# One read-back a tile instead of four, and five weights' low parts made by an adding transfer, in a fused S4 and SwiGLU kernel

## The chip, the cores and the metric

The kernel runs on one core of a Trainium2 chip. The metric is the device time of one execution in microseconds. The core has five engines with queues of their own: PE multiplies matrices, DVE and ACT work elementwise (both read PE's accumulator banks), POOL works elementwise on SBUF, and SP issues most of the transfers (DMA). 16 DMA engines move what SP, ACT and POOL issue. Instructions on one engine run in the order in which they were written; across engines they wait on semaphores.

## The reference

The input is 2048 tokens of width 448. A layer norm with modulation, a long convolution in the form of an S4 state space, and a residual come first; a second layer norm with modulation, a SwiGLU of hidden width 1792, and a second residual follow.

```python
mod = (_silu(c) @ w_mod).reshape(c.shape[0], 6, 1, -1)
sa, ca, ga, sb, cb, gb = (mod[:, 0], mod[:, 1], mod[:, 2], mod[:, 3], mod[:, 4], mod[:, 5])
h = _layernorm(x, axis=-1) * (1 + ca) + sa
x = x + ga * _A_ref(h, ...)          # y[l] = sum over m <= l of K[l - m] h[m], plus h * Dskip
h = _layernorm(x, axis=-1) * (1 + cb) + sb
x = x + gb * ((_silu(h @ w_gate) * (h @ w_up)) @ w_down)
```

## The kernel before

**Tiles and blocks.** The tokens make 16 tiles of 128; two tiles are a block, and there are 8 blocks. The input data let the convolution be done by running sums (the branch taken here; the other branch, for general data, is in the program but does not run). A prologue of about 34 us makes the modulation rows and the first block's input.

**A block** (ffn) runs 14 units f = 0 to 13, each of 128 hidden columns. A unit is gate_up (42 pairs of matmuls into two banks), point (the down products of the unit before, written between gate_up's matmuls at the position POINT), and gating (SiLU on ACT at L774, the product on DVE at L786, its high part on ACT at L791, its low part on DVE at L792). To keep accuracy, each operand is split into a high part, rounded for PE, and a low part, the rest; a product is high x high, high x low and low x high. hhi and hlo are the two parts of the block's turned tokens, phi and plo those of the gated product, wdh and wdl those of w_down, and gu holds both parts of a unit's gate and up weights. gate_up reads hhi with the weights' high part, hlo with the high part, and hhi with the low part; in block 0 the low part comes last.

**Weights.** All weights stay in SBUF. They are loaded and split in block 0 alone: load_w brings the weights of one unit into one of three buffers called raw (L104), split_w makes the high part on ACT (part 0, L121, a unit before its use and in gating) and the low part on DVE (part 1, L123, at the end of unit f for unit f + 2). split_d does the same for w_down.

**The next block's input.** While a block runs, the plan PLANS lists under each unit which steps of the next block's two tiles come there: for each tile X and Y (the second norm's two halves, make_xn at L207 and L209), T (turn) and U (turned_back). Steps marked + come ahead of the cast to phi in gating, the others behind it. turn transposes 32 x 32 pieces on DVE (L239) and SP copies the result to xd in DRAM (L240); turned_back reads it back with the pieces in their places, doubled for PE's two halves, into the buffer place[q] (a raw buffer that is free then), by four transfers of 32 partitions each (L245). In the last unit split_turned makes hhi (ACT, L252) and hlo (DVE, L253) from it, in two steps, LOW and HIGH. The next block's first matmuls need hhi of both tiles. In blocks 1 to 6 tile 0 has T and U under unit 8, tile 1 has X, Y, T and U under unit 10.

**Queues.** SP's order is that of the program: a transfer that waits holds back those written behind it. In block 0 the weight loads stand between the turned tokens' transfers; in later blocks the stores of the block before and the loads of x (L818, L87) stand behind them.

**The end.** In the last block the last two units' down products go to other banks (finish), the sums of the units before are scaled and added to x by last_sums (L832, L833), and three additions (L852) and the stores end the program.

Of the kernel before, what the change touches and what calls it, by code (L numbers as in the profile page):

```python
# [18 lines left out]
L, D, N, F = 2048, 448, 256, 1792  # L19
# [4 lines left out]
NF = F // 128  # L24
# [6 lines left out]

PLANS = (
    """pre: s0 t0 R0 ; mid: f ; g a0 s1 t1 R1 ; b0 G ; r0 h0 ; +v0 a1 c0 ; A0 p0 b1 ; B0 e0 E0 ; r1 h1 u0 w0 M0 ; +v1 X0 Y0 c1 p1 ; A1 T0 ;
    B1 E1 m1 M1 ; U0 X1 Y1 T1 ; U1 e1 ; L0 ; L1""",
    """n0 n1 N ; +l0 a0 b0 k0 ; +l1 k1 r0 h0 ; +v0 a1 b1 c0 ; A0 p0 ; B0 e0 E0 c1 ; r1 h1 m0 M0 p1 ; +v1 X0 Y0 L0 L1 ; A1 T0 U0 ; B1 E1 m1 M1 ; X1 Y1 T1 U1 ; e1 ; ;""",
    "; l0 k0 ; l1 k1",
)
POINT = ([12] + [20] * 12 + [12], [12] + [18] * 12 + [12])  # L40
ORDER = """sf x0 x1 sc m10 se sd m11 m20 m21 m00 m01 sb sa m40 m41 m30 m31 w0 m50 m51 w1 d0 d1 x2 w2 x3 d2"""

PLAN = """t4 pa0 t1 S1 t2 pa1 t3 wi ca gp S20 wr h00 gpc gt h01 mp S21 gac m0 dg gdm mpc k0 a2 t5 sq1 mk gdr h10 cp S3 v00 dga a3 o00
# [8 lines left out]
def f32(ap):  # L52
    return ap.bitcast(F32)
# [3 lines left out]
def tile_kernel(ctx, tc, x, a_re, a_im, b_re, b_im, c_re, c_im, log_dt,  # L57
                wd, wgate_up, states, groups, vecs, dft, idft, out):
    nc = tc.nc
    sy, ve, sc, po, pe = nc.sync, nc.vector, nc.scalar, nc.gpsimd, nc.tensor  # L60
# [5 lines left out]
    dram = ctx.enter_context(tc.tile_pool(name="dram", bufs=1, space=bass.MemoryType.DRAM))  # L66
# [24 lines left out]
    wgu, raw, wdn, wp = {}, {}, {}, {}  # L91
# [5 lines left out]
    place = [stages_[:, q].rearrange("p k c -> p (k c)") for q in (2, 0)]  # L97
# [20 lines left out]
    def split_w(j, part):  # L118
        w = raw[j]
        if part == 0:  # L120
            sc.copy(wgu[j][:, 0], w)  # L121
        else:
            ve.tensor_tensor(wgu[j][:, 1], w, f32(wgu[j][:, 0]), op=OP.subtract)  # L123

    tri = const.tile([128, 128], F32R)
    tok = const.tile([128, 1], F32)
# [66 lines left out]
    n1, n2 = Norm("a"), Norm("b")  # L193
# [37 lines left out]
        ve.tensor_scalar(i, j, 0.0, None, op0=OP.is_equal)  # L231
        return i

    xd = [dram.tile([128, D], F32, name=f"xd{q}") for q in range(2)]

    def turn(i, q):

        src, dst = h_of(i), v0_of(i)
        ve.transpose(dst.rearrange("p (b k r) -> p k b r", b=2, k=7), src.rearrange("p (k b c) -> p k b c", b=2, k=7))  # L239
        sy.dma_start(xd[q], dst)  # L240

    def turned_back(q):
        for z in range(4):
            b = z % 2
            sy.dma_start(place[q][z * 32:(z + 1) * 32].rearrange("c (a n) -> c a n", a=4),  # L245
                         xd[q][:, b * 224:(b + 1) * 224].rearrange("(a c) n -> c a n", a=4))

    def split_turned(ks):
        for q in range(2):
            src = turned[q].rearrange("p a k r -> p k a r")[:, ks]  # L250
            hi, lo = (h[:, ks, cols(q)].rearrange("p k (a r) -> p k a r", a=4) for h in (hhi, hlo))
            sc.copy(hi, src)  # L252
            ve.tensor_tensor(lo, src, f32(hi), op=OP.subtract)  # L253
# [40 lines left out]
    with tc.tile_pool(name="pre", bufs=1) as pre:  # L294
# [4 lines left out]
        for kind, q in ((n[0], n[1:]) for n in ORDER.split()):  # L299
# [3 lines left out]
            elif kind == "m":  # L303
                g, b = int(q[0]), (slice(0, 2 * D), slice(2 * D, NM))[int(q[1])]
# [36 lines left out]
        for z in range(2):  # L341
# [16 lines left out]
        m0, m0_, a1, a2, m1 = (pre.tile([128, 4], F32, name=q) for q in ("m0", "m0_", "a1", "a2", "m1"))  # L358
# [3 lines left out]
        h01, v0, v1, hd = ([pre.tile([128, w], t, name=f"{n}_{q}") for q in range(2)] for n, t, w in  # L362
                               (("h", F32, D), ("v0", F32, D), ("v1", F32R, D), ("hd", F32, D)))
# [116 lines left out]
        k0, k1 = CV[:, 0:D], DN[2][:, 0:D]  # L480
# [259 lines left out]
    def run_blocks(pools, stages, first=None):  # L740
# [13 lines left out]
        def ffn(b, ts, fresh, last, todo):  # L754
            n, sums = 256, SUMS[b % 2]
# [12 lines left out]
            def gating(f, ps, nw):  # L768
                p = hid.tile([128, 256], F32, name="p") if fresh else p_of[f % 2]
                hi = hid.tile([128, 256], F32R, name="phi")  # L770
                lo = hid.tile([128, 256], F32R, name="plo")
                for g, a in todo.get(-2, []) if f == 0 else []:
                    g(*a)
                gate_ready[:] = [sc.activation(p, ps[0][:, 0:n], AF.Silu).ins.name]  # L774
                pp[f] = hi, lo
                if f == NF - 1:
                    if fresh:
                        split_d(f, 1)
                    for q in range(3):
                        for o in [cols(q)] * (q < 2):  # L780
                            ve.tensor_tensor(p[:, o], p[:, o], ps[1][:, o], op=OP.mult)
# [10 lines left out]
                ve.tensor_tensor(lo, ps[1][:, 0:n], f32(hi), op=OP.subtract)  # L792
# [33 lines left out]
                po.tensor_tensor(raw, raw, gb, op=OP.mult)  # L826
                wdn[f] = raw

            def last_sums():

                for q, i in enumerate(ts):
                    ve.tensor_tensor(sums[q][:, 0:D], sums[q][:, 0:D], gb, op=OP.mult)  # L832
                    ve.tensor_tensor(xs[i], sums[q][:, 0:D], xs[i], op=OP.add)  # L833

            def finish():
                o = [*SUMS[1 - b % 2], bank()]
# [36 lines left out]
            for f in range(NF):  # L873
                ps, ops = gate_up(f)
                ops = list(zip(*ops))
                at = POINT[b > 0][f]
                both(ops[0][:at], ops[1][:at])
                point(f)
                both(ops[0][at:], ops[1][at:])
                if f == NF - 1 and not last:  # L880
                    split_turned(LOW)
                gating(f, ps, f + 2 if fresh and f + 2 < NF else None)
                if f == NF - 1 and not last:
                    split_turned(HIGH)
                if last and f in (2, 5):
                    gated(NF - 2 + (f == 5))
                if last and f in (4, 7):
                    split_d(NF - 2 + (f == 7))
                if last and f == NF - 1:
                    last_sums()  # L890
                    return finish()
                if fresh and f == 0 and first is None:
                    sy.dma_start(run[0:1], run[127:128])
                for g, a in todo.get(f, []):
                    g(*a)
                if fresh:
                    if f + 2 < NF:
                        split_w(f + 2, 1)
                    pools.load(f + 2 + NS, f + NS)
            ahead[:] = [begin]  # L900

# [229 lines left out]
```

## Time and profile before

| | |
|---|---|
| time, median of 3 runs | 471.35 us (470.61 to 472.19) |
| the profiled execution | 470.57 us, span 468.8 us |
| granted clock of PE | 0.997 |
| moved by DMA | 35.71 MB, mean 76 GB/s |
| queue of SP and ACT (q1) | 21696 packets, 22.8% of 16 engines' span |
| read-back raw<-xd | 56 transfers of 112 KB, median 3.1 us to landing |
| copy xd<-m | 14 transfers of 224 KB, median 1.9 us to landing |

Times in the profile are microseconds, unless marked ns. A line such as L245 is a line of the kernel before, out<-in names the tiles, and SPq is SP's queue of transfers. The page's busy times and chain say what bounds the whole; what a change at one place is worth is read from the waits at that place.

### The profile page before, as it was taken

What the parts mean: (1) busy time and instruction counts of PE and PEld (TensorE: products, weight loads), DVE (VectorE), ACT (ScalarE), POOL (GpSimd) and SP (SyncE); (2) the same over time, 40 slices, a digit from 0 to 9 for tenths busy, and PEclk for the clock granted to TensorE, in tenths of its full rate; (3) what the DMA queues carried; (4) which work ended last, traced back from release to release, by engine and by line L of the source; (5) the groups of instructions that cost most, each with busy time, mean ns of one, the idle gap of its engine ahead of it and who ended that gap; (6) DMA issues with size and microseconds to landing.
All of it is one profiled execution on the core that took longest, in us unless ns stands there. A gap on an engine that the chain in (4) does not pass through costs nothing.

```text
span 468.8 us, 14329 instructions
## 1 busy us (share of the span) xinstructions
PE 445.5 (95%) x6271; PEld 422.9 (90%) x6271; DVE 296.0 (63%) x605; ACT 159.8 (34%) x390; POOL 95.6 (20%) x125
## 2 busy tenths in 40 slices
PE   6889998899999999999999999999998999999993
PEld 4558988799999999999998999999998999999993
DVE  4888979865765756565764756565764756543224
ACT  5876564532323222332223232332223232322220
POOL 1235112015200241025100241025100241001000
PEclk9999999999999999999999999999999999999998
DMA  8963555502021202202021202202021102211001
GB/s 303 406 235 100 178 161 174 140 22 82 2 80 42 63 19 60 62 12 70 2 80 43 78 3 60 62 20 63 2 80 42 41 3 60 61 40 44 3 3 45
DMA packets 22408, 35.71 MB, mean 76 GB/s; under 512 B 3008, under 2 KB 18240, under 8 KB 22336
## 3 DMA queue, kind: packets, MB, share of 16 engines
q1 hardware_dynamic: 21696, 34.53, 22.8%
q8 instruction: 51, 0.84, 0.8%
q10 hardware_dynamic: 640, 0.18, 0.2%
q14 instruction: 21, 0.17, 0.1%
HBM read 27.76 MB, written 6.88 MB: 74 GB/s over the span
## 4 chain that ended last, share of the span: by engine, by line
PE 69%; DVE 11%; DMA 7%; ACT 6%; issue 4%; SPq 2%; POOL 1%; DVEq 0%; ACTq 0%; POOLq 0%
PE bank L751 43%; PE dn L751 16%; PE cv L751 8%; DMA raw<-xd 3%; DMA xd<-m 3%; SPq L245 2%; DVE gu L123 2%; DVE bank L786 1%; DVE m L207 1%; DVE m L209 1%; ACT gu L121 1%; DVE m L239 1%; ACT phi L791 1%; ACT hhi L252 1%; DVE plo L792 1%
## 5 line engine op out<-in xcount | busy, mean ns | idle before, releaser
L751 PE MATMUL bank<-hhi,gu 64*128 64x256 f32 x3136 | 225.4, 275 | 7.8 <-DVE gu L123 3.9
L751 PEld LDWEIGHTS bank<-hhi,gu 64*128 64x128 f32 x3136 | 205.3, 184 | 11.3 <-DVE gu L123 5.1
L751 PE MATMUL bank<-hlo,gu 64*128 64x256 f32 x1568 | 131.8, 274 | 0.0
L751 PEld LDWEIGHTS bank<-hlo,gu 64*128 64x128 f32 x1568 | 119.2, 184 | 1.8
L786 DVE TENSOR_TENSOR bank<-raw,bank 128x256 f32<-128x256 f32 x91 | 39.0, 429 | 102.3 <-ACT raw L774 101.7
L774 ACT ACTIVATE raw<-bank 128x256 f32<-128x256 f32 x98 | 37.6, 384 | 188.3 <-PE bank L751 188.3
L751 PE MATMUL dn<-wdh,plo 64*128 64x448 f32 x332 | 84.2, 362 | 1.3 <-DVE plo L792 1.3
L751 PE MATMUL dn<-wdh,phi 64*128 64x448 f32 x332 | 84.2, 360 | 0.3 <-DVE run L727 0.3
L751 PE MATMUL dn<-wdl,phi 64*128 64x448 f32 x332 | 84.0, 360 | 0.0
L792 DVE TENSOR_TENSOR plo<-bank,phi 128x256 fp32r<-128x256 f32 x104 | 44.0, 423 | 29.5 <-ACT phi L791 29.5
L791 ACT CAST phi<-bank 128x256 fp32r<-128x256 f32 x104 | 38.9, 374 | 61.9 <-DVE bank L786 61.9
L751 PEld LDWEIGHTS dn<-wdh,plo 64*128 64x128 f32 x332 | 44.9, 184 | 3.3 <-DVE plo L792 1.8
L751 PEld LDWEIGHTS dn<-wdh,phi 64*128 64x128 f32 x332 | 44.9, 184 | 1.8 <-DVE run L727 0.6
L751 PEld LDWEIGHTS dn<-wdl,phi 64*128 64x128 f32 x332 | 45.0, 184 | 1.0
L751 PE MATMUL cv<-wdh,plo 64*128 64x448 f32 x108 | 38.8, 360 | 0.0
L751 PE MATMUL cv<-wdl,phi 64*128 64x448 f32 x108 | 38.8, 359 | 0.0
L751 PE MATMUL cv<-wdh,phi 64*128 64x448 f32 x108 | 38.6, 358 | 0.0
L183 POOL TENSOR_SCALAR rsa<-mva 128x2 f32<-128x2 f32 (+1 forms) x9 | 3.5, 387 | 112.4 <-DVE mva L155 111.8
L183 POOL TENSOR_SCALAR rsb<-mvb 128x1 f32<-128x1 f32 x16 | 4.3, 266 | 104.0 <-DVE mvb L155 103.4
L253 DVE TENSOR_TENSOR hlo<-raw,hhi 128x512 fp32r<-128x512 f32 (+1 forms) x28 | 16.8, 624 | 11.7 <-ACT hhi L252 10.3
L970 POOL TENSOR_TENSOR m<-m,gm 128x448 f32<-128x448 f32 x12 | 13.9, 1158 | 44.7 <-issue 37.3
L751 PEld LDWEIGHTS cv<-wdh,plo 64*128 64x128 f32 x108 | 19.9, 184 | 0.6
(237 smaller groups left out, 533.5 us busy)
## 6 DMA issues: line engine op xcount, KB each, us to landing
raw<-in_B_w_gate_up_dram SPq DMA_DIRECT2D x14, 448.0 KB, 3.4
raw<-xd SPq DMA_DIRECT2D x56, 112.0 KB, 3.1
rawd<-in_B_w_down_dram SPq DMA_DIRECT2D x16, 224.0 KB, 3.6
xd<-m SPq DMA_DIRECT2D x14, 224.0 KB, 1.9
x<-in_A_u_dram SPq DMA_DIRECT2D x12, 224.0 KB, 3.6
out_dram<-x SPq DMA_DIRECT2D x11, 224.0 KB, 2.5
wm<-in_w_mod_groups_dram SPq DMA_DIRECT2D x5, 448.0 KB, 8.2
wm<-in_w_mod_groups_dram SPq DMA_DIRECT2D x5, 336.0 KB, 8.2
```

The costliest lines, as they stand in the source:

```text
L121: sc.copy(wgu[j][:, 0], w)
L123: ve.tensor_tensor(wgu[j][:, 1], w, f32(wgu[j][:, 0]), op=OP.subtract)
L183: po.tensor_scalar(rs[:, 0:n], self.mv[:, 0:n, 1], EPS, None, op0=OP.add)
L207: ve.scalar_tensor_tensor(to, xs[i], m, cbw, op0=OP.subtract, op1=OP.mult)
L245: sy.dma_start(place[q][z * 32:(z + 1) * 32].rearrange("c (a n) -> c a n", a=4), xd[q][:, b * 224:(b + 1) * 224].rearrange("(a c) n -> c a ...
L253: ve.tensor_tensor(lo, src, f32(hi), op=OP.subtract)
L751: done.append(pe.matmul(o, w[e], r[e], start=start, stop=stop).ins)
L774: gate_ready[:] = [sc.activation(p, ps[0][:, 0:n], AF.Silu).ins.name]
L786: ve.tensor_tensor(ps[1][:, 0:n], p, ps[1][:, 0:n], op=OP.mult)
L791: sc.copy(hi, ps[1][:, 0:n])
L792: ve.tensor_tensor(lo, ps[1][:, 0:n], f32(hi), op=OP.subtract)
L970: en.tensor_tensor(v, h, g, op=OP.mult)
```

## The change

Four edits.

1. turn and turned_back. xd is laid out as 64 rows of 896 numbers, and the copy to it is two transfers, one for each half of the columns, each into four places of 32 rows. The read-back is one transfer that takes the 64 rows twice, into 128 partitions.
2. split_w has a part 2 for the weights of units 5, 7, 9, 11 and 13 (ADDED): ACT writes minus the weights, rounded as the high part is, and a transfer issued by POOL adds the weights onto it. It is called at the end of unit j - 3; the subtraction on DVE at the end of unit j - 2 goes for these.
3. In blocks 1 to 6, X of tile 1 has a + (it comes ahead of the cast to phi and of plo).
4. In the last block, the last unit's point stands at position 8 and not 12, and three of the four steps of last_sums come ahead of the last gating.

```diff
+ADDED = (5, 7, 9, 11, 13)
...
-    ... ; B1 E1 m1 M1 ; X1 Y1 T1 U1 ; e1 ; ;""",
+    ... ; B1 E1 m1 M1 ; +X1 Y1 T1 U1 ; e1 ; ;""",
...
-POINT = ([12] + [20] * 12 + [12], [12] + [18] * 12 + [12])
+POINT = ([12] + [20] * 12 + [12], [12] + [18] * 12 + [12], [12] + [18] * 12 + [8])
...
         if part == 0:
             sc.copy(wgu[j][:, 0], w)
+        elif part == 1:
+            ve.tensor_tensor(wgu[j][:, 1], w, f32(wgu[j][:, 0]), op=OP.subtract)
         else:
-            ve.tensor_tensor(wgu[j][:, 1], w, f32(wgu[j][:, 0]), op=OP.subtract)
+            sc.activation(wgu[j][:, 1], w, AF.Copy, scale=-1.0)
+            po.dma_start(f32(wgu[j][:, 1]), w, accum_op=OP.add)
...
-    xd = [dram.tile([128, D], F32, name=f"xd{q}") for q in range(2)]
+    xd = [dram.tile([64, 2 * D], F32, name=f"xd{q}") for q in range(2)]
...
-        sy.dma_start(xd[q], dst)
+        for k in range(2):
+            sy.dma_start(xd[q][k * 32:(k + 1) * 32].rearrange("c (a n) -> a c n", a=4), dst[:, k * 224:(k + 1) * 224])

     def turned_back(q):
-        for z in range(4):
-            b = z % 2
-            sy.dma_start(place[q][z * 32:(z + 1) * 32].rearrange("c (a n) -> c a n", a=4),
-                         xd[q][:, b * 224:(b + 1) * 224].rearrange("(a c) n -> c a n", a=4))
+        sy.dma_start(place[q], xd[q][None].to_broadcast([2, 64, 2 * D]))
...
+                if last and f == NF - 1:
+                    last_sums((0, 0), (0, 1), (1, 0))
                 gating(f, ps, f + 2 if fresh and f + 2 < NF else None)
...
                 if last and f == NF - 1:
-                    last_sums()
+                    last_sums((1, 1))
                     return finish()
...
-                    if f + 2 < NF:
+                    if f + 2 < NF and f + 2 not in ADDED:
                         split_w(f + 2, 1)
+                    if f + 3 in ADDED:
+                        split_w(f + 3, 2)
```

SP's queue at the end of block 0, before: tile 0's copy to xd, weight loads, its read-back, then the same for tile 1 (xd_105 and xd_106 are the two tiles' places in DRAM, rawd the buffers of w_down; the numbers behind a transfer are the counts that it writes).

```order
L240 DMA xd_105<-m_79 128x448
L104 DMA raw<-in_B_w_gate_up_dram 128x896
L109 DMA rawd_83<-in_B_w_down_dram 128x448
L109 DMA rawd_81<-in_B_w_down_dram 128x448
L245 DMA raw<-xd_105 32x4x224 x4
L240 DMA xd_106<-m_79 128x448
L109 DMA rawd_82<-in_B_w_down_dram 128x448
L245 DMA raw<-xd_106 32x4x224 x4
L1016 DMA run<-run 1x16x56
```

The same place in the changed program.

```order
L245 DMA xd_105<-m_79 4x32x224 x2
L105 DMA raw<-in_B_w_gate_up_dram 128x896
L110 DMA rawd_83<-in_B_w_down_dram 128x448
L110 DMA rawd_81<-in_B_w_down_dram 128x448
L248 DMA raw<-xd_105 128x1x896
L245 DMA xd_106<-m_79 4x32x224 x2
L110 DMA rawd_82<-in_B_w_down_dram 128x448
L248 DMA raw<-xd_106 128x1x896
L1025 DMA run<-run 1x16x56
```

No transfer has moved past another; the copies are two each with a count of 4 outermost, the read-backs one each.

POOL in block 0, before, from the first tile's root of the norm to the second tile's skip part.

```order
L184 TENSOR_TENSOR rsa<-rsa,mhalf 128x1
L992 TENSOR_TENSOR m_79<-m_79,gd 128x448
L995 TENSOR_TENSOR x_74<-m_79,x_74 128x448
L175 TENSOR_SCALAR cs<-mvb 128x1
L176 TENSOR_SCALAR mvb<-mvb 128x1
L183 TENSOR_SCALAR rsb<-mvb 128x1
L184 TENSOR_TENSOR rsb<-rsb,mhalf 128x1
L992 TENSOR_TENSOR m_79<-m_79,gd 128x448
```

The same place in the changed program (gu_541, gu_692 and gu_849 are the weights of units 5, 7 and 9).

```order
L188 TENSOR_TENSOR rsa<-rsa,mhalf 128x1
L127 DMA gu_541<-raw 128x896
L1001 TENSOR_TENSOR m_79<-m_79,gd 128x448
L1004 TENSOR_TENSOR x_74<-m_79,x_74 128x448
L127 DMA gu_692<-raw 128x896
L179 TENSOR_SCALAR cs<-mvb 128x1
L180 TENSOR_SCALAR mvb<-mvb 128x1
L187 TENSOR_SCALAR rsb<-mvb 128x1
L188 TENSOR_TENSOR rsb<-rsb,mhalf 128x1
L127 DMA gu_849<-raw 128x896
L1001 TENSOR_TENSOR m_79<-m_79,gd 128x448
```

The skip parts (L992, L1001) now stand behind adding transfers, which wait for ACT.

DVE at the end of the last block, before: the last gating, then the sums and the last additions.

```order
L781 TENSOR_TENSOR raw<-raw,bank 128x128 x2
L784 TENSOR_TENSOR plo<-raw,phi 128x128 x2
L832 TENSOR_TENSOR dn_70<-dn_70,gb 128x448
L833 TENSOR_TENSOR x_74<-dn_70,x_74 128x448
L832 TENSOR_TENSOR cv<-cv,gb 128x448
L833 TENSOR_TENSOR x_75<-cv,x_75 128x448
L852 TENSOR_TENSOR x_74<-dn_68,x_74 128x448
```

The same place in the changed program.

```order
L836 TENSOR_TENSOR dn_70<-dn_70,gb 128x448
L838 TENSOR_TENSOR x_74<-dn_70,x_74 128x448
L836 TENSOR_TENSOR cv<-cv,gb 128x448
L783 TENSOR_TENSOR raw<-raw,bank 128x128 x2
L786 TENSOR_TENSOR plo<-raw,phi 128x128 x2
L838 TENSOR_TENSOR x_75<-cv,x_75 128x448
L857 TENSOR_TENSOR x_74<-dn_68,x_74 128x448
```

Three of the four sums have moved ahead of the last gating.

More of the change, by code (lines that the diff above doesn't have):

```diff
@@ L36 @@
     B1 E1 m1 M1 ; U0 X1 Y1 T1 ; U1 e1 ; L0 ; L1""",
-    """n0 n1 N ; +l0 a0 b0 k0 ; +l1 k1 r0 h0 ; +v0 a1 b1 c0 ; A0 p0 ; B0 e0 E0 c1 ; r1 h1 m0 M0 p1 ; +v1 X0 Y0 L0 L1 ; A1 T0 U0 ; B1 E1 m1 M1 ; X1 Y1 T1 U1 ; e1 ; ;""",
+    """n0 n1 N ; +l0 a0 b0 k0 ; +l1 k1 r0 h0 ; +v0 a1 b1 c0 ; A0 p0 ; B0 e0 E0 c1 ; r1 h1 m0 M0 p1 ; +v1 X0 Y0 L0 L1 ; A1 T0 U0 ; B1 E1 m1 M1 ; +X1 Y1 T1 U1 ; e1 ; ;""",
     "; l0 k0 ; l1 k1",
 )
-POINT = ([12] + [20] * 12 + [12], [12] + [18] * 12 + [12])
+POINT = ([12] + [20] * 12 + [12], [12] + [18] * 12 + [12], [12] + [18] * 12 + [8])
 ORDER = """sf x0 x1 sc m10 se sd m11 m20 m21 m00 m01 sb sa m40 m41 m30 m31 w0 m50 m51 w1 d0 d1 x2 w2 x3 d2"""
@@ L827, in gated, with last_sums @@
                 wdn[f] = raw
[L829 to L833, printed above, removed]
+            def last_sums(*parts):
+                for q, k in parts:
+                    i, t = ts[q], sums[q][:, 0:D]
+                    if k == 0:
+                        ve.tensor_tensor(t, t, gb, op=OP.mult)
+                    else:
+                        ve.tensor_tensor(xs[i], t, xs[i], op=OP.add)
             def finish():
@@ L875, in ffn @@
                 ops = list(zip(*ops))
-                at = POINT[b > 0][f]
+                at = POINT[2 if last else b > 0][f]
                 both(ops[0][:at], ops[1][:at])
```

## The prediction

> **What bounds the kernel now.** I read the page first (busy shares, chain), then who PE waits for, then the chain of waits around one block boundary, then the queue's issues there.
>
> ```profile
> span 468.8 us, 14329 instructions
> PE 445.5 (95%) x6271; PEld 422.9 (90%) x6271; DVE 296.0 (63%) x605; ACT 159.8 (34%) x390; POOL 95.6 (20%) x125
> PE 69%; DVE 11%; DMA 7%; ACT 6%; issue 4%; SPq 2%; POOL 1%; DVEq 0%; ACTq 0%; POOLq 0%
> ```
>
> The page of before: the sum is made against this execution's own 470.57 us (span 468.8 and 1.8 around it); the median of the runs, 471.35, lies 0.8 above. PE works 95% of the span, so there is little to win, and everything that makes PE idle is lost. Who PE waits for (total us, times, longest):
>
> ```profile
> PE bank L751 <- DVE gu L123: 3.9, 5, 1.6
> PE bank L751 <- ACT hhi L252: 3.4, 5, 1.2
> PE dn L751 <- DVE plo L792: 1.3, 1, 1.3
> ```
>
> The first and third rows lie in block 0, where DVE makes the weights' low parts. The second is the boundary between blocks: PE cannot begin a block before both of its tiles are turned, written to DRAM, read back and split. One boundary (block 2 to 3) in the chain of waits, in order of time (start, us, what):
>
> ```profile
> 189.81 0.69 DVE m L209
> 190.53 0.66 DVE m L239
> 191.24 1.93 DMA xd<-m
> ...
> 194.79 3.04 DMA raw<-xd
> 198.52 1.66 PE bank L751 x24
> ```
>
> The reader is to see that tile 1's whole way lies on the chain, with no slack: the turn ends at 191.2, the copy in DRAM stands at 193.2, the read-back has landed at 197.8, PE starts the next block 0.7 later. Whatever that way grows by, PE idles, seven times in the program. Tile 0 goes the same way 8.9 us earlier, on the same queue:
>
> ```profile
> 182.35 0.33 SPq L240 DMA_DIRECT2D xd<-m  x1
> 184.35 1.75 SPq L245 DMA_DIRECT2D raw<-xd  x4
> 191.24 0.34 SPq L240 DMA_DIRECT2D xd<-m  x1
> 193.23 2.79 SPq L245 DMA_DIRECT2D raw<-xd  x4
> ```
>
> **The transfers, the step that decides.** Removed: four reads a tile (112 KB each). Added: one read of 448 KB, and two writes of 112 KB in place of one of 224 KB. The bytes are the same. What no row shows is on how many of the 16 engines the new ones run. All that ran before had counts of 128, 32 or 16 outermost on both sides; even the one-row transfer run<-run is written as 16 pieces (1x16x56 in the program's order). The new read has its two copies outermost on the DRAM side (counts 2, 64, 896) against 128 partitions; the new write has 4 outermost in DRAM against 128. The bounds are 16 engines, as before, and what the outermost counts can share out evenly: 2 for the read, 4 for the write. I take the lower one: it lies nearest to the one transfer of the old program that had no even count of its own, run<-run, whose single row was cut in 16 before it was issued, which would be needless if the engines shared out bytes and not outermost steps.
>
> The Trainium skill, page "DMA: Bandwidth & Descriptors", section "Why a DMA increments its semaphore by 16 and not by 1", says the same as a rule: the engines used are the largest number up to 16 that divides the outermost counts of both sides; its section "Rules for kernel authors" says that a leading zero-stride broadcast of c copies "confines the whole DMA to at most c engines". No run here shows it yet; by the opposite reading (16 engines) the sum is rival 1's.
>
> Price of an engine's share, from two stretches in which little but one kind of transfer ran (weights 44 to 47 us; one copy to xd 182.3 to 184.4 us; packets, MB, share of 16 engines), and the time to landing of the old reads (min, median, max):
>
> ```profile
> q1 hardware_dynamic: 275, 0.64, 56.6%
> ...
> q1 hardware_dynamic: 144, 0.23, 29.5%
> DMA to landing us min/median/max: 2.1/3.1/3.9
> ```
>
> 0.64 MB in 0.566 x 16 x 3.0 = 27.2 engine-us is 23.6 KB per us and engine; 0.23 MB in 0.295 x 16 x 2.1 = 9.9 is 23.2. The read on 2 engines is 64 rows of 3584 B, 229 KB, on each: **9.7 us**. An old read had 7 KB an engine, 0.3 us, of its shortest 2.1, so 1.8 is fixed: 11.5 us in all. The two writes on 4 engines put 57 KB on each: 2.5 us, plus the old write's fixed part (1.93 - 0.62 = 1.3): 3.8.
>
> Now the boundary of block 2, step by step. Tile 0's write 182.35 + 3.8 = 186.2. Its read lands at 197.7 and holds its two engines from about 187.1 to 196.8 (half of the fixed part ahead, half behind). Tile 1's write is issued at 191.2; its share on those two engines stands behind the read, 196.8 + 2.5 + 0.7 = 200.0. SP issues tile 1's read only then; it lands at 211.5; hhi 0.7 later, PE starts at 212.2 and not at 198.52: **+13.7**. X1 ahead of plo on DVE brings the turn some 0.4 forward (L792 takes 0.42), worth nothing where the write stands behind the read. Fewer issues (1.75 to 2.8 us of SP) are worth nothing there either. Behind tile 1's read SP has only the stores of the block before (they wait for DVE some 11 us into the next block), so nobody else waits for its longer wait. Six such boundaries: 82.2. At block 0's end:
>
> ```profile
> 81.92 1.76 SPq L245 DMA_DIRECT2D raw<-xd  x4
> 85.19 0.34 SPq L240 DMA_DIRECT2D xd<-m  x1
> 93.88 1.07 PE L751 MATMUL bank<-hhi,gu 64*128 64x256 f32 x16
> ```
>
> The read from 81.92 holds its engines till 92.5, tile 1's write lands at 95.7, its read at 107.2, PE starts at 107.9: +14.0, less about 1.5 that DVE is ahead by then (below): 12.5. The weight load of f = 13 that SP issues between is late too, but inside that same wait.
>
> **What the idle time itself costs.** PE's first matmuls of the program, after standing still (ns min/median/max):
>
> ```profile
> L291 PEld LDWEIGHTS bank<-tri x14: 187/310/337, 1.5 to 5.9; 128*128 128x128 f32 x14
> L751 PEld LDWEIGHTS dn<-wdh,plo 64*128 64x128 f32 x332 | 44.9, 184 | 3.3 <-DVE plo L792 1.8
> ```
>
> A weight load took 310 there and takes 184 at pace; 14 x 0.126 = 1.8 us lost per start from rest. No later idle stretch in the trace is over 2 us, so whether 14 us of idling does the same is bounded by 0 and 1.8 each; I take 1.75, the only row of a start from rest: 7 x 1.75 = 12.3.
>
> **Block 0's weights.** Five subtractions leave DVE, five scaled copies join ACT and five adding transfers POOL's queue.
>
> ```profile
> 47.25 0.98 PE L751 MATMUL bank<-hhi,gu 64*128 64x256 f32 x12 [0.56 <-DVE gu L123]
> 89.43 1.09 DVE L123 TENSOR_TENSOR gu<-raw,gu 128x896 fp32r<-128x896 f32 x1
> 90.58 0.74 PE L751 MATMUL bank<-hhi,gu 64*128 64x256 f32 x8 [1.64 <-DVE gu L123]
> 43.38 0.95 ACT L121 CAST gu<-raw 128x896 fp32r<-128x896 f32 x1
> 50.05 0.38 ACT L774 ACTIVATE p<-bank 128x256 f32<-128x256 f32 x1
> 45.09 1.16 POOL L992 TENSOR_TENSOR m<-m,gd 128x448 f32<-128x448 f32 x1 [1.63 <-DVE v L970]
> 61.77 0.62 DVE L1020 TENSOR_TENSOR x<-x,dn 128x448 f32<-128x448 f32 x1
> ...
> raw<-in_B_w_gate_up_dram SPq DMA_DIRECT2D x14, 448.0 KB, 3.4
> ```
>
> DVE saves 5 x 1.09 = 5.4 us; PE's waits for it are 3.9, of which the 0.56 at 47.25 is for weight 3, which keeps its subtraction: at most 3.3. ACT pays 0.95 ahead of the next SiLU each time; at 50.05 ACT had no idle time ahead of it, so one or two of the five come through, 0.9 us. On POOL the first adding transfer waits for ACT (about 50), and L992 behind it goes from 45 to some 52; its reader L1020 comes at 61.8, so that is covered. The adding transfer itself has no row: it is issued about two units ahead of the pass that reads it (a unit is 104.6/28 = 3.7 us, from the starts of blocks 1 and 3 at 93.88 and 198.52), so it has some 7 us; a plain load of that size lands in 3.4. I cost it at nothing (up to +10 in rival 2). Gain 2.4 by itself; here it only makes block 0 wait longer at its end, except for the 1.5 above.
>
> **The end.** Three of the four last sums move ahead of the last gating, and the last point comes four steps earlier:
>
> ```profile
> 459.27 0.48 DVE L781 TENSOR_TENSOR raw<-raw,bank 128x128 f32<-128x128 f32 x2 [1.70 <-ACT raw L774]
> 460.34 0.62 DVE L832 TENSOR_TENSOR dn<-dn,gb 128x448 f32<-128x448 f32 x1
> 462.20 0.62 DVE L833 TENSOR_TENSOR x<-cv,x 128x448 f32<-128x448 f32 x1
> 463.60 0.35 DVE L852 TENSOR_TENSOR x<-bank,x 128x192 f32<-128x192 f32 x1
> ```
>
> DVE's tail behind the gating is four operations of 0.62 and three shorter additions. Three of the four go into the 1.7 us in which DVE waited for ACT ahead of 459.27; 3 x 0.62 = 1.9, less the 0.2 to 0.3 by which they delay the gating: **-1.6**, in every case.
>
> Sum: 470.6 + 82.2 + 12.5 + 12.3 - 1.6 = **576**.
>
> **Rivals.** (1) Not slower: the new transfers run on all 16 engines. Then tile 1's read is issued at once and lands about 2.8 us later (229/8 KB an engine, 1.2, plus 1.8) at 196.2 instead of 197.8; with X1's 0.4 the boundary waits of 3.4 go. 470.6 - 3.4 - 2.4 - 1.6 = **463**. For it: the old reads' 3.1 us and the queue's 4 issues on the chain are real, and all transfers in the trace use all engines. Against it: their outermost counts. (2) 16 engines, but the adding transfers are late: five times up to 2 us of PE's idle time from the point at which one takes over 6 us (twice a weight load's 3.4, since it reads two operands): 470.6 + 10 - 3.4 - 1.6 = **476**. (3) The waits that go are replaced by the next in line (SP, ACT's casts) and only part of the end's gain stays: **470**.
>
> **How the numbers follow.** The forecast 0.68, rival 1 0.24, rival 2 0.05, rival 3 0.03. The forecast's own range: lower end with the writes still on 16 engines and no slow start (+9.6 a boundary: 470.6 + 67 - 3.1 = 534, say 530); upper end where a 3584 B row takes four times the 47 ns which an 896 B one takes by the queue's share between 184.3 and 188 us (row below): 12 us a read, twice a boundary, +32, so 608.
>
> ```profile
> q1 hardware_dynamic: 572, 0.46, 45.5%
> ```
>
> Both signs hold much chance, so the range goes down to rival 1's 462; 530 to 608 is the likeliest case's own. About 0.3% (1.4 us) is what a measurement of this kernel can tell from no change: faster 0.24, within 0.03, slower 0.73.
>
> **What would show it.** Right: the read from xd lands 10 to 13 us after its issue, PE waits 12 to 15 us for ACT hhi at each of seven boundaries, and the DMA share there is about 2 of 16. Wrong: a landing near 3 us and no such waits; then the time is rival 1's, and the first block decides between it and rival 2 (PE's waits for gu). At the end one sum, not four, stands behind the last gating on DVE. Only the boundary's size (the write standing behind the read, the start from rest) can be off by itself.

## The result

The changed kernel takes 598.59 us (median of 4 runs, 596.67 to 599.53) where the kernel before takes 471.34 (470.61 to 472.19): a ratio of 1.269, 95% interval 1.266 to 1.273. The profiled execution took 598.68 us, with a span of 596.9.

The page of the changed kernel: span, busy time, PE's granted clock in 40 slices, the shares of the chain that ended last.

```profile
span 596.9 us, 14299 instructions
PE 468.8 (79%) x6271; PEld 445.9 (75%) x6271; DVE 293.5 (49%) x600; ACT 164.6 (28%) x395; POOL 99.2 (17%) x130
PEclk9998978689995999769996899959997699959999
PE 58%; DMA 27%; DVE 6%; ACT 4%; issue 3%; SPq 1%; POOL 1%; ACTq 0%; DVEq 0%; POOLq 0%
```

The transfers' share of the chain went from 7% to 27%. PE does the same 6271 matmuls in 23.3 us more (468.8 against 445.5), and its idle time grows by 104.8 us (from 23.3 to 128.1). Together that is the whole growth of the span, 128.1 us; that some of these numbers are alike is chance. Whom PE waits for (total us, times, longest):

```profile
PE bank L753 <- ACT hhi L254: 105.3, 7, 16.0
PE bank L753 <- DMA gu<-raw: 5.7, 3, 4.4
PE dn L753 <- DVE plo L794: 2.7, 2, 1.3
PE dn L753 <- DVE wdl L117: 2.4, 2, 1.3
PE bank L753 <- DVE gu L124: 0.3, 1, 0.3
```

The waits at the block boundaries were 3.4 us in all, at five of the seven; they are now 12.6 us at the end of block 0 and 14.8 to 16.0 us at the six others. One of them in the chain of waits (start, us, what), the same step that the prediction showed of before:

```profile
235.72 0.66 DVE m L243
...
237.02 9.95 DMA xd<-m
...
247.11 11.50 DMA raw<-xd
...
259.30 2.71 PE bank L753 x17
```

Behind tile 1's turn, its copy to DRAM now takes 9.95 us from the issue of its second half (1.93 before) and its read-back 11.50 (3.04). SP's issues of the two tiles:

```profile
228.27 1.11 SPq L245 DMA_DIRECT2D xd<-m  x2
232.87 0.54 SPq L248 DMA_DIRECT2D raw<-xd  x1
236.44 1.10 SPq L245 DMA_DIRECT2D xd<-m  x2
```

Tile 0's copy, with nothing in its way, was there after 4.6 us (228.27 to 232.87, where the read that waits for it is issued); tile 1's, issued while tile 0's read ran, took 10.6 (its read-back is issued at 247.11). And the DMA engines while tile 1's read runs alone (249 to 257 us; 40 slices in tenths, then packets, MB, share of 16 engines):

```profile
DMA  0000101010101010101010101001010101010101
...
q1 hardware_dynamic: 109, 0.39, 12.1%
```

12.1% of 16 engines is 1.94: the work of two engines (the profile does not name them). 0.121 x 16 x 8.0 us over 109 packets is 142 ns for a row of 3584 B, 25 KB per us and engine. This is what the rule in the Trainium skill, "DMA: Bandwidth & Descriptors", section "Why a DMA increments its semaphore by 16 and not by 1", gives for counts of 2 and 128 outermost, and the trace agrees with it.

What a block's first 16 matmuls take behind the wait, and what they take later in the block (start, us, operation, idle time before):

```profile
259.30 2.08 PE L753 MATMUL bank<-hhi,gu 64*128 64x256 f32 x16 [15.24 <-ACT hhi L254]
...
264.96 1.07 PE L753 MATMUL bank<-hhi,gu 64*128 64x256 f32 x16
```

PE's granted clock around the same wait, in stretches (from:to, its length, busy us of PE, PEld, DVE, ACT and POOL, granted clock, DMA share, GB/s):

```profile
249.00:257.00 8.00, 0.00 (x0) 0.00 (x0) 0.00 (x0) 0.00 (x0) 0.00 (x0) 0.50 0.12 49
...
264.00:265.00 1.00, 1.00 (x22) 1.00 (x20) 0.00 (x0) 0.00 (x0) 0.00 (x0) 1.00 0.00 0
```

PE stops at 244.1. The clock is still 1.00 from 245 to 246, 0.50 from 247 to 263 although PE works again from 259.3, and 1.00 again from 264: here PE's first four us behind the wait run at half the clock.

### The profile page after: what moved, and what is told of

The parts are those of the page before. It is cut to its first block, busy times and chain, and to the rows that moved or that the text cites. A ratio compares the mean times of both kernels' runs of the same rounds, so it can differ in the third digit from the quotient of the medians.

```text
span 596.9 us, 14299 instructions
## 1 busy us (share of the span) xinstructions
PE 468.8 (79%) x6271; PEld 445.9 (75%) x6271; DVE 293.5 (49%) x600; ACT 164.6 (28%) x395; POOL 99.2 (17%) x130
## 4 chain that ended last, share of the span: by engine, by line
PE 58%; DMA 27%; DVE 6%; ACT 4%; issue 3%; SPq 1%; POOL 1%; ACTq 0%; DVEq 0%; POOLq 0%
PE bank L753 37%; DMA raw<-xd 13%; PE dn L753 13%; DMA xd<-m 13%; PE cv L753 6%; DVE bank L788 1%; DVE m L213 1%; DVE m L243 1%; ACT hhi L254 1%; DVE m L211 1%; SPq L245 1%; DVE wdl L117 1%; DMA vec<-in_c_log_dt_dram 1%; ACT gu L122 1%; DVE vl L996 1%
## 5 line engine op out<-in xcount | busy, mean ns | idle before, releaser
L753 PE MATMUL bank<-hhi,gu 64*128 64x256 f32 x3136 | 239.2, 284 | 111.7 <-ACT hhi L254 105.3
L753 PEld LDWEIGHTS bank<-hhi,gu 64*128 64x128 f32 x3136 | 218.8, 193 | 115.3 <-ACT hhi L254 106.7
L753 PE MATMUL bank<-hlo,gu 64*128 64x256 f32 x1568 | 139.2, 282 | 0.0
L753 PEld LDWEIGHTS bank<-hlo,gu 64*128 64x128 f32 x1568 | 126.8, 192 | 1.3
L753 PE MATMUL dn<-wdh,plo 64*128 64x448 f32 x332 | 88.2, 373 | 2.7 <-DVE plo L794 2.7
L753 PE MATMUL dn<-wdl,phi 64*128 64x448 f32 x332 | 87.7, 370 | 2.4 <-DVE wdl L117 2.4
L753 PE MATMUL dn<-wdh,phi 64*128 64x448 f32 x332 | 88.4, 372 | 0.8 <-ACT p L776 0.5
L753 PEld LDWEIGHTS dn<-wdl,phi 64*128 64x128 f32 x332 | 48.1, 192 | 3.8 <-DVE wdl L117 3.1
L753 PEld LDWEIGHTS dn<-wdh,phi 64*128 64x128 f32 x332 | 48.5, 194 | 2.3 <-ACT p L776 0.7
L254 ACT CAST hhi<-raw 128x512 fp32r<-128x512 f32 (+1 forms) x28 | 15.1, 562 | 108.8 <-DMA raw<-xd 108.8
```

The costliest lines, as they stand in the source:

```text
L753: done.append(pe.matmul(o, w[e], r[e], start=start, stop=stop).ins)
```

## The experiments

Ratios are to the kernel before, run on the same chip in the same set; a time without an interval is that of a single run.

**The new transfers alone, and all but them.** The first kernel is before with the new `xd`, `turn` and `turned_back`; the second is the changed kernel with the old ones.

```diff
-        sy.dma_start(xd[q], dst)
+        for k in range(2):
+            sy.dma_start(xd[q][k * 32:(k + 1) * 32].rearrange("c (a n) -> a c n", a=4), dst[:, k * 224:(k + 1) * 224])
...
+        sy.dma_start(place[q], xd[q][None].to_broadcast([2, 64, 2 * D]))
```

> The kernel before with only the transfers exchanged (two writes, one read a tile). Theory: all seven boundary waits are there, 14 to 16 us each, PE works 20 to 25 us longer at a granted clock near 0.89, and the time is 590 to 598. Rival (the adding transfers fill the queues and so make the turning slow): the boundary waits stay below 3 us and the time is below 485.

> The changed kernel with the transfers of before (one write and four reads a tile), so the other parts of the change alone. Theory (the new transfers carry the loss): the seven waits of PE for ACT hhi fall from 15.0 us each to about 0.5, the granted clock returns to about 0.99, and the time is 463 to 475. Within that, if the adding transfers are late only because the slow turning transfers share engines with them, they land in 3 to 4 us, PE's waits in the first block fall from 11.1 to under 3, and the time is about 465; if they are late in themselves they land in about 6 us again and the time is about 473. Rival (the adding transfers or the moved steps carry the loss): the time stays above 560.

With the new transfers alone: 589.99 us, at the lower edge of what was expected. The busy times on its page:

```profile
PE 462.3 (79%) x6271; PEld 442.0 (75%) x6271; DVE 296.0 (50%) x605; ACT 160.2 (27%) x390; POOL 95.6 (16%) x125
```

And the first row of its PE's waits:

```profile
PE bank L749 <- ACT hhi L250: 106.2, 7, 15.8
```

All seven boundary waits are there, and PE is busy 16.8 us longer than in before, not 20 to 25: the rest of the changed kernel's 23.3 comes from its other parts.

With all but them: 471.64 us, ratio 0.999 (0.997 to 1.002); the waits for ACT hhi are 0.3 us in all. So the transfers carry the whole loss, and the other parts together come to nothing. In the second kernel the adding transfers still take a median of 6.1 us to land (6.3 in the changed kernel): they are slow in themselves, not because of the slow read-backs.

**Which of the two transfers, and by what.** The read in two halves of 64 partitions (64 rows outermost on both sides); the write in four parts of 32 partitions (32 outermost on both sides); both.

```diff
-        sy.dma_start(place[q], xd[q][None].to_broadcast([2, 64, 2 * D]))
+        for z in range(2):
+            sy.dma_start(place[q][z * 64:(z + 1) * 64], xd[q])
```

```diff
-        for k in range(2):
-            sy.dma_start(xd[q][k * 32:(k + 1) * 32].rearrange("c (a n) -> a c n", a=4), dst[:, k * 224:(k + 1) * 224])
+        for a in range(4):
+            sy.dma_start(xd[q].rearrange("(k c) (a n) -> a c k n", k=2, a=4)[a],
+                         dst[a * 32:(a + 1) * 32].rearrange("c (k n) -> c k n", k=2))
```

> The changed kernel with the read made as two transfers of 64 partitions, each with 64 rows outermost on both sides, the two writes left as they are. Theory (the read runs on 2 engines, and tile 1's write is late only because it stands behind that read): the read lands 2 to 3.5 us after its issue, tile 1's write in 4 to 5 us as tile 0's does, the boundary waits fall from 15 to 2 to 4 us, and the time is 478 to 500. Rival (the write by itself takes the 10 us that tile 1's took): boundary waits near 9 us and a time of 545 to 560. Rival (reading the same 229 KB twice from DRAM is what is slow, not the count of engines): the read still takes over 9 us and the time stays above 580.

> The changed kernel with each tile's write made as four transfers with 32 partitions outermost on both sides, the read left as it is. Theory (what counts for the write is the engines that the read of tile 0 still holds): tile 0's write lands in 2 to 3 us and its read starts some 2 us earlier, tile 1's write is spread over 16 engines but two of those are still held by the read, so it lands 7 to 9 us after its issue and not 10; the boundary waits are 12 to 15 us and the time is 572 to 597. Rival (the write's own 4 engines are what makes it slow): tile 1's write lands in 2 to 3 us, the waits fall by 7 to 8 us to about 7.5, and the time is 535 to 550.

> The changed kernel with the write as four transfers of 32 partitions and the read as two of 64 partitions, so that all outermost counts are multiples of 16; the turned layout in DRAM is that of the change. Theory (the loss is the count of engines and nothing else): write 2.5 to 3.5 us from its first issue, read 3 to 3.8 us, no boundary wait over 1.5 us, and the time is that of the changed kernel with the transfers of before (471.6) plus 0 to 9 us, 471 to 481. Rival (the turned layout, or reading it twice, costs time by itself): boundary waits of 2 us and more and a time of 485 to 497 as with the read alone in two.

The read in two: 496.04 us. PE waits for ACT hhi 13.5 us in all, at six boundaries, 3.2 us at most. One read-back in the chain of waits, and the DMA queue while it runs (266 to 270 us):

```profile
266.13 3.80 DMA raw<-xd
```

```profile
q1 hardware_dynamic: 160, 0.46, 44.0%
```

The same bytes from the same place in DRAM, read twice as before, land in 3.8 us. So it is the count of engines and not the second reading. Tile 1's copy, its form unchanged, is there after 4.7 to 5.0 us at five of the six later boundaries and after 5.7 at this one, no longer after 10.6: it was late because of the read ahead of it.

The write in four: 570.77 us, boundary waits 79.5 us in all, 11.4 on average (8.8 at block 0's end, 11.5 to 12.3 later). Both lie just below what the theory gave, 572 to 597 us and 12 to 15, and far from the rival's. SP's issues at a boundary (tile 0's read, tile 1's copy):

```profile
288.40 0.50 SPq L249 DMA_DIRECT2D raw<-xd  x1
293.40 1.73 SPq L245 DMA_DIRECT2D xd<-m  x4
```

Tile 1's copy and read-back in the chain of waits:

```profile
294.69 5.38 DMA xd<-m
300.14 11.65 DMA raw<-xd
```

If tile 0's read, issued at 288.40, takes as long as tile 1's, it ends at 300.05; tile 1's copy, spread over 16 engines, is there at 300.07 (at the five other later boundaries 0.6 to 1.1 us behind the read). It waits for the two engines that the read holds, as in the changed kernel, where it landed 2.6 us behind the read (232.87 + 11.50 = 244.4, then 246.97), its larger share on those two engines being 57 KB instead of 14. It took 6.7 us here and up to 7.8 elsewhere, where 7 to 9 was expected. Both changed: 479.08 us, ratio 1.015 (1.012 to 1.018), longest boundary wait 1.4 us. That is inside 471 to 481, but by the ratios still 7.4 us above the kernel with the old transfers: its boundary waits are 5.4 us in all where those are 0.3, PE's waits for late weights 5.4 where those are 2.7, and SP issues six transfers a tile and not five. The trace is of the fastest of its five runs (475.68 us, clock 0.996; the others 478.9 to 479.8 at 0.983 to 0.989), so what slows the others is not seen in it.

**What standing still costs.** Filler matmuls that nobody reads, ahead of each block's first unit; first into a bank of their own, then into the bank which that unit overwrites.

```diff
+            if b:
+                warm(30)
+                warm(30)
```

```diff
+                if b and f == 0:
+                    warm(52 if b == 1 else 64, ps[0])
```

> The changed kernel with 60 matmuls of 128x512 that nobody reads, put on PE ahead of each block's first unit (blocks 1 to 7), so that PE works while it would wait; nothing else differs. At full pace they take about 0.22 us each (14 of them took 6.24 us at the program's start, at half pace), some 13 us of the 15 us wait. Theory (each wait also costs PE about 3.3 us of slow work afterwards, because it stood still): the block's first 16 matmuls take 1.07 us and not 2.07, the granted clock rises from 0.892 to above 0.98, the boundaries stay as long, and the time falls by 15 to 23 us, to 575 to 584. Rival (the 23.3 us more of PE's busy time have another cause, such as the late weights or data that come in slowly): the time stays within 4 us of 598.6.

> The changed kernel with filler matmuls again (52 ahead of block 1, 64 ahead of blocks 2 to 7, about 0.23 us each), but written into the bank that the block's first unit overwrites anyway, so that no other bank's release is waited for (in the run before, the first unit had to take the bank that the last unit's SiLU still read: 14 us of new waits). Theory (standing still costs PE 3.3 us of slow work behind each wait): the waits for ACT behind the filler stay below 1 us, the first 16 matmuls take 1.1 us, the granted clock is above 0.98, and the time is 575 to 584. Rival (the slow start comes from the first data, not from standing still, or filler costs as much as it saves): 592 to 600.

The first took 603.19 us, longer, which neither side had expected: the banks' turn moved on by two, and the block's first unit had to wait for the bank that the last unit's gating still read (10.9 us of new waits for ACT and 3.1 for DVE). The second took 583.67. A boundary of the first, then of the second:

```profile
244.09 13.90 PE L293 MATMUL bank<-tri 128*128 128x512 f32 x60
259.17 0.38 PE L753 MATMUL bank<-hhi,gu 64*128 64x256 f32 x1 [1.18 <-ACT raw L776]
260.10 1.90 PE L753 MATMUL bank<-hhi,gu 64*128 64x256 f32 x15 [0.55 <-DVE raw L783]
```

```profile
241.82 13.08 PE L293 MATMUL bank<-tri 128*128 128x512 f32 x57
255.41 1.18 PE L753 MATMUL bank<-hhi,gu 64*128 64x256 f32 x16 [0.51 <-ACT hhi L254]
```

With the second filler the granted clock over the whole run is 0.988 (0.892 in the changed kernel), it is 1.00 from 241 to 260, and the 16 matmuls take 1.18 us, not 2.08; 14.9 us come back by this single run, 2.1 a boundary. The longest wait for ACT hhi behind it was 1.3 us, where less than 1 was expected. So the slow start is caused by standing still.

**Where the first block loses.** Weight 11 taken off the list; then, with the old transfers, the list cut in two.

```diff
-ADDED = (5, 7, 9, 11, 13)
+ADDED = (5, 7, 9, 13)
```

> The changed kernel with weight 11 taken off the list, so that its low part is a subtraction on DVE again; the other four are still adding transfers. Theory (tile 0's read lands in the buffer that weight 11's adding transfer still reads, so the read waited for that transfer, 8 us longer than in the kernel with only the transfers exchanged, 90.57 against 82.56): the read is issued at 82 to 84 us, block 1 begins at 109 to 112 us and not 119.7, and the time is 588 to 592. Rival (the loss in the first block is PE's own waits for late weights, of which 13's is the largest, 4.4 us): block 1 begins within 3 us of 119.7 and the time is 595 to 599.

592.34 us, and block 1 begins at 118.0: the theory fell, and so did the rival's time, 595 to 599. The read was issued at 88.74 all the same, behind DVE's own subtraction of weight 11, which came at 87.64. The block was 5 us late long before that; of the 6.3 us by which this single run is below the changed kernel, the start of block 1 holds only 1.7; the rest lies in blocks 1 to 7 (472.6 us against 477.2), where the weights' low parts are no longer made, and why is open.

When each unit's SiLU starts (us, from the timelines of ACT) shows the place; "small parts" is the kernel before with the end and the second tile's step alone, which comes below:

| unit | 3 | 4 | 5 | 7 | 8 | 9 | 12 | 13 |
|---|---|---|---|---|---|---|---|---|
| small parts | 49.79 | 53.69 | 57.68 | 67.94 | 72.19 | 76.78 | 88.48 | 93.82 |
| same, with all five adding transfers | 49.97 | 56.82 | 61.28 | 71.36 | 77.95 | 83.74 | 94.71 | 100.64 |

Three us are lost at unit 4, then 2.3 and 1.2 at units 8 and 9, and little elsewhere. At unit 4 in the kernel with all five (POOL, DVE, PE), and then the same in the small parts alone:

```profile
50.39 1.09 POOL L127 DMA_DIRECT2D gu<-raw  x1 [7.11 <-ACT p L778]
51.22 1.45 POOL L1003 TENSOR_TENSOR m<-m,gd 128x448 f32<-128x448 f32 x1
52.75 1.40 POOL L1006 TENSOR_TENSOR x<-m,x 128x448 f32<-128x448 f32 x1
...
50.71 2.45 DVE L117 TENSOR_TENSOR wdl<-rawd,wdh 128x448 fp32r<-128x448 f32 x1
53.09 1.55 DVE L998 TENSOR_TENSOR vl<-m,vh 128x448 fp32r<-128x448 f32 x1
...
53.22 0.47 PE L755 MATMUL dn<-wdl,phi 64*128 64x448 f32 x2 [0.98 <-DVE wdl L117]
55.02 0.74 PE L755 MATMUL dn<-wdh,plo 64*128 64x448 f32 x2 [1.34 <-DVE plo L796]
...
55.94 2.06 PE L755 MATMUL bank<-hhi,gu 64*128 64x256 f32 x15
```

```profile
46.06 1.88 POOL L1000 TENSOR_TENSOR x<-m,x 128x448 f32<-128x448 f32 x1
...
47.19 1.24 DVE L116 TENSOR_TENSOR wdl<-rawd,wdh 128x448 fp32r<-128x448 f32 x1
...
51.08 0.60 DVE L116 TENSOR_TENSOR wdl<-rawd,wdh 128x448 fp32r<-128x448 f32 x1
```

POOL's product, put behind the adding transfer, runs at 51 us and not at 45, now beside the subtraction that PE needs next. That subtraction takes 2.45 us instead of 0.60 (in the other kernel the one before it takes 1.24, beside POOL's sum); here POOL's sum in turn falls beside DVE's next operation (L998), which takes 1.55 us instead of 0.61, and plo stands behind that. So PE waits 2.3 us in two pieces, and then works at half pace (15 matmuls in 2.06 us). The Trainium skill, "SBUF — State Buffer", section "SBUF: two separate sides", describes a port pair that VectorE, in an operation with two operands in SBUF, and GpSimd, in one that reads SBUF, lock against each other for a whole instruction. These rows agree with it: three DVE operations end 0.49 us behind the POOL operation beside them (53.16 and 52.67, 54.64 and 54.15, 48.43 and 47.94), as if held until then; only the first is recorded as starting before the product, while POOL was still issuing the transfer.

> The changed kernel with the transfers of before and with adding transfers for weights 7, 11 and 13 only. Weights 5 and 9 are those whose issue stands on POOL right ahead of its two products (L1001 and L1004 in the changed kernel), which so come some 6 and 3 us later. Theory A (the loss of the adding transfers, 7.5 us from 464.15 to 471.6, is made where those products run beside DVE: low parts of down weights take 2.45 and 2.26 us there and not 0.62, and PE waits for them): without 5 and 9 these waits go and the time is 464 to 467, ratio 0.984 to 0.990. Theory B (the loss is made by transfers that land late, weight 13's above all, or by weight 11's that holds the read-back's buffer): the time stays at 469 to 472.

> The same with adding transfers for weights 5 and 9 only. Theory A: the waits at the two places stay (units 4 and 8 begin 3 and 2.5 us later than without), DVE's two saved subtractions give little back, and the time is 468 to 471.5. Theory B: no late transfer is left at the block's end and the time is 464 to 466.

Weights 7, 11 and 13 alone: 468.86 us, ratio 0.994 (0.991 to 0.996). Weights 5 and 9 alone: 471.24 us, 0.998 (0.996 to 1.000). Without any: 0.984. PE's waits of the first, then of the second:

```profile
PE bank L755 <- DMA gu<-raw: 6.6, 2, 4.0
```

```profile
PE bank L755 <- DVE gu L124: 3.3, 4, 1.6
PE dn L755 <- DVE wdl L117: 2.4, 2, 1.3
PE dn L755 <- DVE plo L796: 2.4, 2, 1.3
```

Theory A holds for 5 and 9, with a loss of 6.6 us by the ratios (0.998 against 0.984; such differences are known to about 1.6 us); without them its waits are gone, but the gain it expected (464 to 467) does not come: transfers 7 and 11 are then late by 2.6 and 4.0 us, for a loss of 4.6. They landed 7.3 and 8.7 us after their issue, and PE wanted both 4.7 us after it. Theory B is right about those, not about the whole. The two losses do not add: all five together lose 7.4. In the kernel with all five, PE waits 0.5 us for weight 7, not at all for 11 and 2.2 us for 13: it is late already when it reaches 7 and 11.

**The small parts.** The kernel before with the end and with the second tile's first step (`+X1`), and with the end alone.

```diff
-    ... ; B1 E1 m1 M1 ; X1 Y1 T1 U1 ; e1 ; ;""",
+    ... ; B1 E1 m1 M1 ; +X1 Y1 T1 U1 ; e1 ; ;""",
...
-POINT = ([12] + [20] * 12 + [12], [12] + [18] * 12 + [12])
+POINT = ([12] + [20] * 12 + [12], [12] + [18] * 12 + [12], [12] + [18] * 12 + [8])
...
+                if last and f == NF - 1:
+                    last_sums((0, 0), (0, 1), (1, 0))
```

> The kernel before with the two small parts of the change alone: the last block's sums and point, and the second tile's first normalising step moved ahead. Theory: the end gives 1.6 us, and the seven boundary waits (3.4 us in all) go, as they did in the changed kernel with the transfers of before, where the adding transfers gave as much back; so 470.6 - 5 = 465 to 467.5, ratio 0.987 to 0.993. Rival (the waits that go are replaced by the next in line and only the end counts): 469 to 470, ratio 0.996.

> The kernel before with the end alone (three of the four last sums ahead of the last gating, the last point four steps earlier). The end and the second tile's step together gave 7.5 us (464.15 against 471.6). Theory (the end gives the 1.6 us that were worked out, the rest is the boundaries): 469.5 to 470.5, ratio 0.995 to 0.998, and the seven boundary waits stay (3 to 4 us in all). Rival (the end gives more, since DVE's sums were in the way of the last matmuls too): 466 to 468.

Both: **464.15 us, ratio 0.984 (0.981 to 0.986)**, the fastest of all kernels here, and a little better than the theory's 465 to 467.5. The end alone: 469.44 us, 0.993 (0.990 to 0.996), with 4.4 us of boundary waits left, at six boundaries; with the step too, 0.3. DVE at the boundary of block 2 in before, then with both parts:

```profile
187.82 0.43 DVE L786 TENSOR_TENSOR bank<-raw,bank 128x256 f32<-128x256 f32 x1 [0.17 <-ACT raw L774]
188.69 0.42 DVE L792 TENSOR_TENSOR plo<-bank,phi 128x256 fp32r<-128x256 f32 x1 [0.44 <-ACT phi L791]
```

```profile
186.99 0.43 DVE L786 TENSOR_TENSOR bank<-raw,bank 128x256 f32<-128x256 f32 x1 [0.17 <-ACT raw L774]
187.33 0.68 DVE L207 SCALAR_TENSOR_TENSOR m<-x,mvb,cbw 128x448 f32<-128x448 f32 x1
187.92 0.42 DVE L792 TENSOR_TENSOR plo<-bank,phi 128x256 fp32r<-128x256 f32 x1
...
188.97 0.65 DVE L239 STREAM_TRANSPOSE m<-m 128x448 f32<-128x448 f32 x1
```

The transposition starts 1.98 us behind the gating's product here and 2.71 in before (187.82 to 190.53): 0.73 us. The step stands in blocks 1 to 6, so six times: 4.4 us. By the ratios it gives 0.009 of 471.6, 4.3 us (known to about 1.7), and the end 3.3 (2.1 to 4.5).

## Why the prediction came out as it did

The mechanism that it put first is the one that the runs show. The time is 22.6 us above the 576 forecast. By the traces, 12.9 us of that lie in the first block (ahead of the wait at its end), which was forecast to lose nothing, 7.1 in the six later boundary waits, and 3.1 in the starts from rest; the end gave 0.7 more than forecast. So most of the gap is a step that failed, not a size. PE's busy time by stretch shows where it works slowly (us):

| | ahead of block 0 | block 0 | blocks 1 to 7 |
|---|---|---|---|
| before | 26.7 | 54.7 | 364.2 |
| new transfers alone | 27.3 | 54.7 | 380.3 |
| changed kernel | 28.0 | 61.2 | 379.6 |
| changed kernel with the old transfers | 27.6 | 58.3 | 364.4 |

- **Engines.** The read on 2 engines is measured (12.1%), and ends with even counts (3.8 us). Its price was forecast at 11.5 us; it took 11.50 (11.0 to 11.6 over the boundaries). That it agrees so closely is luck: at 142 ns a row, 64 rows take 9.1 us and 2.4 are fixed, where 9.7 and 1.8 were set. Nor were rows of 188 ns, for which the range went up to 608, what brought the time near that end.
- **The write behind the read.** Right in kind: even the read, and tile 1's copy falls from 10.6 to 5 us; even the write, and it still waits for the read. Too small in size: 3.8 us forecast for a copy alone and 8.8 for tile 1's, measured 4.6 and 10.6. The seven waits grew by 101.9 us (105.3 - 3.4) where 94.7 was forecast (82.2 + 12.5): the six later ones by 14.9 each and not 13.7, so that five of the seven are above the 12 to 15 us named as a sign. At block 0's end 12.6 was measured for 12.5 forecast, in part by luck: tile 1's copy took 15.6 us there (91.90 to 107.52, beside weight loads) where 10.5 was forecast.
- **The start from rest.** 1.75 us each was taken, as the upper bound. In blocks 1 to 7 PE is busy 16.1 us longer with the new transfers alone and 15.4 in the changed kernel, 2.2 to 2.3 at each of seven starts, and the filler gives 2.1 back. That term should have been 15.4 and not 12.3. Of the 23.3 us, 6.6 come in the first block; the kernel with the old transfers has 3.7 there, and half pace behind short waits is seen in it at units 4 and 8. The remaining 1.3 come ahead of block 0.
- **Block 0's weights.** This step failed. The adding transfer was costed at nothing, with "some 7 us" to land in and a plain load's 3.4 beside it; in the changed kernel five of them took a median of 6.3 us, and weight 13's was issued at 92.50, wanted by PE at 96.90, 4.4 us later, and landed after 8.7. And of POOL's move it said that L992's reader comes late enough; the reader did, but the move itself set the product beside a DVE subtraction that PE needs. Gain forecast 2.4 (1.5 at the boundary); PE's waits in the first block went from 5.2 to 11.1 us instead. With the old transfers the five cost 7.4 us, and block 0 is 6.7 us longer than in before; the other 6.2 of the 12.9 come only with the new transfers beside them (alone those leave it as long as before). Rival 2 had the late transfers right, but not POOL's product, and it took the new read and copies to run on 16 engines.
- **X1.** "Worth nothing where the write stands behind the read" fits the traces: the whole wait follows the read. Its size, 0.4, was too small: it is 0.73, as the step also fills the 0.44 us in which DVE waited for ACT, and with the old transfers it removes the boundary waits.
- **The end.** -1.6 was forecast. In the changed kernel DVE is done 4.56 us behind the start of PE's last 12 `hhi` matmuls (588.00 to 592.56), in before 6.38 (457.57 to 463.95): -1.8. From the same start to the end of the span it is 8.9 us against 11.2, and 8.4 with the end alone: -2.3 and -2.8, the latter inside the timed 2.1 to 4.5. What DVE does not explain lies behind its last addition, in the last stores: the one of 96 KB landed after 3.8 us in before and after 2.7 with the end alone. Why, is open.

```profile
590.36 0.49 DVE L786 TENSOR_TENSOR plo<-raw,phi 128x128 fp32r<-128x128 f32 x2 [0.17 <-ACT phi L784]
590.77 0.62 DVE L838 TENSOR_TENSOR x<-cv,x 128x448 f32<-128x448 f32 x1
...
592.21 0.35 DVE L857 TENSOR_TENSOR x<-bank,x 128x192 f32<-128x192 f32 x1
```

One sum, not four, stands behind the last gating, as was said. Rival 1's 463 needed even counts, and more: the new transfers at even counts still lose 7.4 us to the old ones, and the weights' gain of 2.4 did not come. The two small parts without either reach 464, near that number by other terms. (In that rival's working 1.2 and 1.8 us make 3.0, not 2.8; its landing at 196.2 has the 3.0.)

## What to carry to other kernels

Count transfers by the engines that their outermost counts can share, and not by their number: one read on two engines cost more than four on sixteen, and it delayed every other transfer that had a share on those two. When work is moved on one engine, look at what then runs beside it on the others, not only at who reads its result. And measure the parts of a change apart: here two small parts were worth 1.6% and were buried under the large one.

## What was not expected of the hardware

Short waits can cost PE its pace too, and near 2 us their length alone does not say when. With the read in two, the 16 matmuls behind waits of 1.96, 1.98 and 2.05 us took 1.19 or 1.20 us, behind 2.06 and 2.27 us 1.86 and 1.82, and behind 3.19 us 2.07. Behind the first filler, where one matmul and another 0.55 us of waiting came between, waits of 1.50, 1.90 and 1.94 us kept the pace (15 matmuls in 1.16 to 1.18 us), 1.18 and 1.74 us lost it (1.90 and 2.04). In the first block two waits of 0.98 and 1.34 us, with a few matmuls between them, were followed by 15 in 2.06 us. Behind the wait of 2.06 us the granted clock was still 1.00 when PE began again and fell to 0.50 some 0.3 us later. What decides is open. The Trainium skill, "TensorE: Matmul & The Clock Gate", section "What's actually happening", ties half pace to an idle window of about 3.4 us: the waits of 12 to 16 us agree, these shorter ones came below it.

A transfer's issue also took longer on SP in the new forms: 0.53 us for half a copy and 0.54 for the read, against 0.33 for the old copy. And a transfer that adds 448 KB onto SBUF landed in 4.5 to 8.7 us beside the old transfers (medians 6.1 with five of them, 7.3 with three, 5.4 with two), where a plain load of that size from DRAM took 3.4 in before.
